# A weight-making step rearranged: an early store, two VectorE steps moved ahead, a cast in front of a wait

## The chip, the cores and the metric

The kernel runs on one core of a Trainium2 chip. TensorE multiplies matrices, VectorE (DVE) and ScalarE (ACT) do element work, GpSimd (POOL) does some element work and issues part of the transfers, SyncE (SP) issues the rest. Each engine runs its own queue in order and waits on semaphores for the others. The metric is device time in microseconds; lower is better.

## The reference

Linear attention with random features (`phi(x) = exp(h - max h)`), and behind it two feed-forward layers over 2304 tokens, of width 512 and inner width 2048:

```python
x = attention(q, k, v, omega)                     # [2304, 512]
h = x @ w_in;  x = (max(h, 0) + alpha * min(h, 0)) @ w_out
h = x @ w2_in; out = max(h, 0)**2 @ w2_out
```

The weights are float64 numbers; the result is float32.

## The kernel before, in words

**Products.** Every float32 matrix is held as two parts, a rounded one (`h`) and the rest (`l`), and a product is three TensorE products of such parts. Tokens are three blocks of 768. The 2048 inner columns are eight pairs `p` of 2 x 128. For a pair, the block products of `x @ w_in` are made with seven products in place of eight (a Strassen-Winograd scheme): the weight blocks A21, A22, A11, A12 and four sums S1 to S4 of them stand as eight columns of `wf1`, products 1, 2, 6, 5, 7, 4, 3 follow each other in `pair` (line 840 is the matmul), and in between stand slices of the second product `y` of the pair before (line 1036). Two PSUM banks called `h` serve the seven products in turn, so the second product of a pair (product 2) can begin only when VectorE's line 878 has read the last one (product 3) of the pair before.

**Making weights.** A pair's weights have to be made before it is used: this goes on beside the first token block, one unit a pair. Unit n stands beside pair n-1 and makes `w_in` of pair n and `w_out` of pair n-1. A `Raw` object is 512 KB of float64 words: POOL fetches it (line 128) into one of three buffers `ms`, ScalarE scales the high words (138) and the low words (146) and puts the sign in (153), VectorE shifts (157) and merges (161) to float32. In unit n the four raw rows are called `a`, `b` (the two rows of `w_in`) and `p`, `q` (those of `w_out`, q the last). A buffer is free for the fetch of the raw row three places on when shift and sign have read it, so `q` is fetched once `a` has been shifted. Then `sums` (179) adds S1, S3, S2, S4, `cast1`/`cast2` (`high`, 244, ScalarE) round, `rest1`/`rest2` (`low`, 247, VectorE) subtract, and `keep` (250, SP's queue) writes both parts to DRAM, since blocks 2 and 3 read them again: 1792 KB for `w_in`, 2 x 512 KB for `w_out` a unit.

**What sets the order.** It is written out by hand: `evenly` puts every step of a unit on one of seven stages (`STEPS`), and stage m's instructions are issued just ahead of product m of the pair. Within an engine this order is final. Work of the products themselves (ACT 865 copies out of PSUM, DVE 878, 883, 889 bend and split) stands between. `APART` places four subtractions of `x` (`apart`, 527, POOL) beside the steps 13 to 16 of the attention's second half.

Of the kernel before, what the change touches and what calls it, by code (L numbers as in the profile page):

```python
# [44 lines left out]

MADE = {3: 1, 4: 2, 5: 3, 6: 4, 7: 5, 12: 6, 13: 8, 14: 9, 15: 10, 16: 11, 17: 12, 18: 14, 19: 16, 20: 18}
CASTS = (7, 8, 9, 10)
APART = {13: 4, 14: 6, 15: 5, 16: 3}
CAST = 11
STAGES, SHORT = 18, 10  # L50
STEPS = (2, 5, 7, 10, 12, 15, 17)
# [10 lines left out]
def tile_performer_moe(ctx, tc, qt, kt, qn, kn, vn, omt, w1i, w1o, al, w2i, w2o, out):  # L62
# [27 lines left out]
    A21, A22, A11, A12, S1, S2, S3, S4 = range(8)  # L90
# [9 lines left out]
    ring = {}  # L100
# [85 lines left out]
    def made():  # L186
# [19 lines left out]
        def merge(raw):  # L206
            raw.merge()
            if raw in raws:
                read_out(raw)

        def read_out(raw):
            raws.remove(raw)
            fetch()
# [35 lines left out]
        def keep(key, which, at, tile, queue=nc.sync):  # L249
            queue.dma_start(out=kept[key][which][:, :, at].bitcast(F32), in_=tile.bitcast(F32))  # L250

            if at in (0, slice(0, 7), slice(5, 7)):
                done.add((key, which))

        f1, f2 = tiles["wf1"], tiles["wf2"]
# [16 lines left out]
        def cast1(key, a0, a1):  # L272
            high(first(key, 0, a0, a1), f1[:, a0:a1])

        def rest1(key, a0, a1):
            low(first(key, 1, a0, a1), f1[:, a0:a1], first(key, 0, a0, a1))
# [8 lines left out]
        def evenly(n, n1, n2, todo):  # L285

            def put(step, *what):
                todo[STEPS[step]] += what

            joined = tiles["joined"], tiles["single"].bitcast(I32)  # L290
            put(0, trail)
            put(1, trail)
            if n1:
                a, b = used[n, 0, 0], used[n, 0, 1]
                put(0, a.scale_high)
                put(1, lambda: a.scale_low(joined[0]), a.sign, a.shift, lambda: read_out(a))
                put(2, lambda: merge(a), b.scale_high, lambda: b.scale_low(joined[1]), b.shift)
                put(3, b.sign, lambda: read_out(b), lambda: cast1(n1, A11, S1))
                put(4, lambda: merge(b), lambda: sums((1, 3)), lambda: sums((2, 4)), lambda: rest1(n1, A11, S1))
            if n2:  # L300
                p, q = (lambda: used[n, 1, 1]), (lambda: used[n, 1, 0])
                put(3, lambda: p().scale_high())
                put(4, lambda: p().scale_low(joined[0]))
            if n1:
                put(4, lambda: cast1(n1, A22, A11))
            if n2:
                put(4, lambda: p().sign(), lambda: p().shift(), lambda: read_out(p()), lambda: q().scale_high())
            if n1:
                put(4, lambda: cast1(n1, S1, S3), lambda: rest1(n1, A22, A11))
                put(5, lambda: rest1(n1, S1, S3))  # L310
            if n2:
                put(5, lambda: q().scale_low(joined[1]), lambda: q().sign(), lambda: merge(p()),
                    lambda: q().shift(), lambda: read_out(q()))
            if n1:
                put(5, lambda: cast1(n1, S3, 8))
            if n2:
                put(6, lambda: cast2(n2, 1))
            if n1:
                put(6, lambda: rest1(n1, S3, 8),
                    lambda: keep(n1, 0, slice(0, 7), ring[n1[1] % 2][0][:, :, A22:]))  # L320
            if n2:
                put(6, lambda: merge(q()), lambda: rest2(n2, 1),
                    lambda: tail.extend([lambda: cast2(n2, 0), lambda: rest2(n2, 0)]))
# [199 lines left out]
    def apart(n):  # L523

        of = {T1: (T3, T1), T3: (T2, T3), T2: (T2, T1), T4: (T4, T2)}[n]
        a, b = (in_place(0, m) for m in of)
        nc.gpsimd.tensor_tensor(out=in_place(0, n), in0=a, in1=b, op=ALU.subtract)
# [561 lines left out]
    for n, (layer, k, turn, p) in enumerate(plan):  # L1089
        lead = plan[n + 1] if n + 1 < len(plan) else None  # L1090
        held[p % 2] = layer, p
        reading = lead and lead[:2] != (0, 0) and held[lead[3] % 2] != (lead[0], lead[3])
        if layer:
            making_room.close()
            values(0)
        fill = enumerate(mm2(*before)) if before else iter(())
        full = []
        first, whole = (layer, k) == (0, 0), n < 2
        if n == 0:
            ask(ENDS[0], None)  # L1100
        steps = stepping.pop() if stepping else plain(p) if whole else pair(layer, p)
        for m, got in enumerate(steps, DRAINED if n == 0 else 0):
            if reading and m in (0, 2):
                read(lead[0], lead[3], 0, m // 2)
            if layer and m == 0:
                for part in GROUPS:
                    read_pair(0, 1, part)
            if first and turn:

                upto((p + 1) * STAGES + STAGES * (m + 1) // (8 if whole else 7) + 1, ENDS[0], None)  # L1110
            elif layer == 0 and k and turn * 7 + m > 3:
                upto(end_of(ENDS[k - 1]) + (end_of(ENDS[k]) - end_of(ENDS[k - 1])) * (turn * 7 + m - 3) // (0, 52, 49)[k],
                     ENDS[k], k)
            elif layer == 0 and k and m == 3:
                ask(ENDS[k], k)
            elif (layer, k, turn) == (0, 1, 0) and m < 2:

                onward(ENDS[0], None)
            for what, operand_ in SPLIT.get((n, m), ()):
                what(0, operand_, in_place)  # L1120
            for blk, at in ((n // NPAIR, turn * 7 + m), (n // NPAIR - 1, NPAIR * 7 + turn * 7 + m)):

                if 0 <= blk < BLOCKS:
                    at -= (NPAIR - 1) * 7
                    for what, operand_ in [*(NEXT if blk else LATER).get(at, ()), *TABLE.get(at, ())]:
                        what((blk + 1) % BLOCKS, operand_)
            for rows in full:
                evacuate(ended, y, rows)
            full = []
            for _ in range(FILL[0 if whole else 1][m]):  # L1130
                part, _ = next(fill, (None, None))
                if turn == 0 and part is not None and part in COMPLETE:
                    full.append(COMPLETE[part])
        for part, _ in fill:
            if turn == 0 and part in COMPLETE:
                full.append(COMPLETE[part])
        for rows in full:
            evacuate(ended, y, rows)
        if turn == 0 and not layer:
            y = [py.tile([P, 512], F32, name=f"y{c}") for c in range(NB // P)]  # L1140
        if reading and lead[0] == 0:
            read(lead[0], lead[3], 1, 1)
            read(lead[0], lead[3], 1, 0)
        before = turn, p, *got, y
        ended = k
# [302 lines left out]
```

## Time and profile before

| | |
|---|---|
| median of 3 runs | 882.21 us (881.02 to 882.24) |
| profiled execution | 880.5 us, span 878.7 us |
| PE busy | 867.7 us (99%) |
| DVE, ACT, POOL busy | 676.5, 520.7, 96.7 us |
| granted TensorE clock | 1.00 over the span, that is 2.4 GHz |
| moved by DMA | 228.76 MB, mean 260 GB/s |

The stretches: attention to about 130 us, the eight pairs of the first token block from there to about 262 us (here the weights are made), then the other blocks and the second layer. PE's busy time is modelled at its ends, so a busy share of 99% doesn't say that matmuls follow at their full pace: the start-to-start distance of matmul rows does.

### The profile page before, as it was taken

The page shows a single profiled execution, that of the slowest core. Times are in us where ns is not written, and L with a number is a line of the kernel's source. Part 1 is how long each engine was busy: PE and PEld are TensorE (multiplying, and loading weights), DVE is VectorE, ACT ScalarE, POOL GpSimd, SP SyncE. Part 2 cuts the span into 40 slices and gives each one's busy share as a digit, 9 for nine tenths or more (in the row PEclk, how much of TensorE's full clock was granted, in tenths as well). Part 3 has the DMA queues.
Part 4 walks back from the last instruction along what each step waited for, and adds up shares of the span by engine and source line. Part 5 has one row for each costly group of instructions (what it writes and reads, how often), then busy time and mean ns, then how long its engine had stood idle before and what let it go on. Part 6 is the DMA issues. An engine that isn't in the chain of part 4 may idle for free.

```text
span 878.7 us, 17471 instructions
## 1 busy us (share of the span) xinstructions
PE 867.7 (99%) x6812; PEld 800.0 (91%) x6812; DVE 676.5 (77%) x1117; ACT 520.7 (59%) x1027; POOL 96.7 (11%) x138
## 2 busy tenths in 40 slices
PE   9999999999999999999999999999999999999998
PEld 7998889978888999989999999998899988999887
DVE  4778996888797777788787874669965699757685
ACT  6889886888776666576676643335523245333442
POOL 6642441111101000001000000000000000000000
PEclk9999999999999999999999999999999999999999
DMA  8544305778846999947999975777697687876873
GB/s 288 181 144 154 110 14 213 267 272 332 289 173 243 331 387 380 380 147 280 395 402 394 359 253 181 252 255 281 239 304 253 207 329 252 284 261 224 303 259 142
DMA packets 86898, 228.76 MB, mean 260 GB/s; under 512 B 6688, under 2 KB 19360, under 8 KB 81824
## 3 DMA queue, kind: packets, MB, share of 16 engines
q1 hardware_dynamic: 77248, 192.21, 61.0%
q0 software_dynamic: 9216, 33.56, 10.9%
q10 hardware_dynamic: 352, 1.87, 0.6%
q8 instruction: 54, 0.88, 0.4%
q14 instruction: 28, 0.23, 0.1%
HBM read 170.47 MB, written 57.15 MB: 259 GB/s over the span
## 4 chain that ended last, share of the span: by engine, by line
PE 68%; DVE 2%; ACT 2%; DMA 1%; issue 0%; DVEq 0%; ACTq 0%
PE h L840 22%; PE y L1036 16%; PE sumc L1227 11%; PE spare L840 10%; PE suma L1227 9%; DMA ms<-in_w1o 1%; DMA x<-in_w2i 0%; PE h L1227 0%; DVE xl L501 0%; DVE w L247 0%; DVE c L883 0%; ACT x L1054 0%; DVE wf L161 0%; DVE gl L889 0%; ACT x L138 0%
## 5 line engine op out<-in xcount | busy, mean ns | idle before, releaser
L840 PE MATMUL h<-xh,w 128*128 128x384 f32 x1016 | 288.2, 338 | 3.8 <-DVE c L878 3.2
L840 PEld LDWEIGHTS h<-xh,w 128*128 128x128 f32 x1016 | 186.3, 188 | 9.1 <-DVE c L878 5.7
L1036 PE MATMUL y<-gh,w 128*128 128x512 f32 (+1 forms) x768 | 175.5, 338 | 1.5 <-DVE w L247 1.2
L840 PE MATMUL h<-xl,w 128*128 128x384 f32 x508 | 170.5, 336 | 0.0
L1036 PEld LDWEIGHTS y<-gh,w 128*128 128x128 f32 x768 | 130.5, 188 | 15.2 <-DVE w L247 3.1
L1036 PE MATMUL y<-gl,w 128*128 128x512 f32 (+1 forms) x384 | 102.4, 337 | 0.0
L1242 ACT CAST gh<-g 128x768 fp32r<-128x768 f32 x72 | 56.9, 833 | 74.1 <-PE suma L1227 33.2
L840 PEld LDWEIGHTS h<-xl,w 128*128 128x128 f32 x508 | 95.5, 188 | 2.0
L840 PE MATMUL spare<-xh,w 128*128 128x384 f32 x336 | 91.0, 334 | 0.0
L1244 DVE TENSOR_TENSOR gl<-g,gh 128x768 fp32r<-128x768 f32 x72 | 65.7, 953 | 14.3 <-PE suma L1227 7.1
L1227 PE MATMUL sumc<-w,gh 128*128 128x512 f32 (+1 forms) x296 | 76.6, 379 | 0.0
L1036 PEld LDWEIGHTS y<-gl,w 128*128 128x128 f32 x384 | 67.1, 188 | 9.6
L840 PEld LDWEIGHTS spare<-xh,w 128*128 128x128 f32 x336 | 61.3, 188 | 0.2
L1227 PEld LDWEIGHTS sumc<-w,gh 128*128 128x128 f32 x296 | 52.8, 188 | 9.3
L613 DVE TENSOR_REDUCE mx<-h 128x8 f32<-128x1024 f32 x36 | 44.0, 1223 | 20.8 <-PE h L600 20.2
L878 DVE SCALAR_TENSOR_TENSOR c<-h,sg_sb,s 128x384 f32<-128x384 f32 x66 | 40.5, 614 | 24.3 <-ACT s L865 13.7
L865 ACT ACTIVATE s<-h,sg_sb 128x384 f32<-128x384 f32 x66 | 38.1, 577 | 31.8 <-PE h L840 31.8
L883 DVE SCALAR_TENSOR_TENSOR c<-c,al_sb 128x768 f32<-128x768 f32 x48 | 48.6, 1013 | 9.9 <-ACT c L865 9.9
L840 PE MATMUL spare<-xl,w 128*128 128x384 f32 x168 | 56.1, 334 | 0.0
L1227 PE MATMUL suma<-w,gh 128*128 128x512 f32 x216 | 52.4, 391 | 0.0
L865 ACT ACTIVATE gh<-c,sg_sb 128x768 fp32r<-128x768 f32 x48 | 45.0, 938 | 7.3 <-DVE c L883 6.9
L889 DVE SCALAR_TENSOR_TENSOR gl<-c,sg_sb,gh 128x768 fp32r<-128x768 f32 x48 | 48.5, 1010 | 0.0
(133 smaller groups left out, 1488.5 us busy)
## 6 DMA issues: line engine op xcount, KB each, us to landing
w<-k SPq DMA_DIRECT2D x99, 512.0 KB, 5.2
w<-k SPq DMA_DIRECT2D x39, 1024.0 KB, 5.1
w<-k SPq DMA_DIRECT2D x26, 896.0 KB, 9.0
k<-ms SPq DMA_DIRECT2D x36, 512.0 KB, 7.4
k<-w SPq DMA_DIRECT2D x7, 1792.0 KB, 6.8
k<-w SPq DMA_DIRECT2D x16, 512.0 KB, 6.5
x<-in_w2i POOLq DMA_DIRECT2D x16, 512.0 KB, 6.7
x<-in_w2o POOLq DMA_DIRECT2D x16, 512.0 KB, 7.2
```

The costliest lines, as they stand in the source:

```text
L613: nc.vector.reduce_max(out=mx, in_=pj, axis=AX.X)
L840: nc.tensor.matmul(out, w[:, u, a, cs], tiles[v, b][:, kc], start=start and kc == 0 and j == 0, stop=stop and kc == 1 and j == 2, skip_gro ...
L865: nc.scalar.mul(out=to, in_=of, mul=sg_sb[:, 2 * p + i:2 * p + i + 1])
L878: nc.vector.scalar_tensor_tensor(out=c[:, ts], in0=b, scalar=sign, in1=s, op0=ALU.mult, op1=ALU.add)
L883: nc.vector.scalar_tensor_tensor(out=c, in0=c, scalar=slope, in1=c, op0=ALU.mult, op1=ALU.max)
L889: nc.vector.scalar_tensor_tensor(out=gl[:, i], in0=c, scalar=sign, in1=gh[:, i].bitcast(F32), op0=ALU.mult, op1=ALU.subtract)
L1036: nc.tensor.matmul(y[a0 // 512][:, a0 % 512:a0 % 512 + a1 - a0], u[:, i, c * P:(c + 1) * P], v[:, i, ts], start=first and j == 0 and a0 % ...
L1227: nc.tensor.matmul(to[c] if v == 3 or banks else to[c][:, :QW], (l if v == 2 else h)[:, r, c * P:(c + 1) * P], both(r) if v == 3 else w[:, ...
L1242: nc.scalar.copy(out=h[:, r], in_=f[:, r])
L1244: nc.vector.tensor_tensor(out=l[:, r], in0=f[:, r], in1=h[:, r].bitcast(F32), op=ALU.subtract)
```

## The change

Four things change. The store of a unit's `w_in` parts is cut in two: columns 0 to 3 (A22, A11, A12) are stored in step 4, as soon as their rests are there, the four sums in step 6. VectorE's merge of row `b` and the first rest come one step sooner (step 3 in place of 4). ScalarE's casts of A22 and of the sums S1, S2 move in front of the scaling of `p`'s low words and of `q`'s high words, and the cast of S3, S4 in front of `q`'s low words. And one `apart` (T4) leaves step 16 of the attention for the first product of pair 1.

```diff
-APART = {13: 4, 14: 6, 15: 5, 16: 3}
+APART = {13: 4, 14: 6, 15: 5}
...
-            if at in (0, slice(0, 7), slice(5, 7)):
+            if at in (0, slice(0, 7), slice(3, 7), slice(5, 7)):
                 done.add((key, which))
...
+            def save(a0, a1):
+                keep(n1, 0, slice(a0, a1), ring[n1[1] % 2][0][:, :, A22 + a0:A22 + a1])
...
-                put(3, b.sign, lambda: read_out(b), lambda: cast1(n1, A11, S1))
-                put(4, lambda: merge(b), lambda: sums((1, 3)), lambda: sums((2, 4)), lambda: rest1(n1, A11, S1))
+                put(3, b.sign, lambda: read_out(b), lambda: cast1(n1, A11, S1), lambda: merge(b),
+                    lambda: rest1(n1, A11, S1))
+                put(4, lambda: sums((1, 3)), lambda: sums((2, 4)), lambda: cast1(n1, A22, A11))
...
-                put(4, lambda: p().scale_low(joined[0]))
-            if n1:
-                put(4, lambda: cast1(n1, A22, A11))
+                put(4, lambda: p().scale_low(joined[0]), lambda: p().sign(), lambda: p().shift(), lambda: read_out(p()))
+            if n1:
+                put(4, lambda: cast1(n1, S1, S3), lambda: rest1(n1, A22, A11), lambda: save(0, 3))
+                put(5, lambda: rest1(n1, S1, S3), lambda: cast1(n1, S3, 8))
             if n2:
-                put(4, lambda: p().sign(), lambda: p().shift(), lambda: read_out(p()), lambda: q().scale_high())
-            if n1:
-                put(4, lambda: cast1(n1, S1, S3), lambda: rest1(n1, A22, A11))
-                put(5, lambda: rest1(n1, S1, S3))
-            if n2:
+                put(4, lambda: q().scale_high())
...
-            if n1:
-                put(5, lambda: cast1(n1, S3, 8))
...
-                put(6, lambda: rest1(n1, S3, 8),
-                    lambda: keep(n1, 0, slice(0, 7), ring[n1[1] % 2][0][:, :, A22:]))
+                put(6, lambda: rest1(n1, S3, 8), lambda: save(3, 7))
...
+            if (n, m) == (1, 0):
+                apart(T4)
```

The later lines of `after` are two lower than before (878 is 876, 865 is 863, 179, 247, 161, 157, 244, 138 stay). On **VectorE**, in the middle of a unit (here the one that makes pair 4; `t,joined` is row a or p, `t,ma` row b or q, `w_0_102` the eight weight columns), before:

```order
L161 ISA wf_100<-t,joined 128x1024
L157 TENSOR_SCALAR t<-ms_2697 128x512
L878 SCALAR_TENSOR_TENSOR c<-h,sg_sb,s 128x384
L161 ISA wf_100<-t,ma 128x1024
L179 TENSOR_TENSOR wf_100<-wf_100 128x256 x4
L247 TENSOR_TENSOR w_0_102<-wf_100,w_0_102 128x512
L157 TENSOR_SCALAR t<-ms_2698 128x512
L247 TENSOR_TENSOR w_0_102<-wf_100,w_0_102 128x256
L247 TENSOR_TENSOR w_0_102<-wf_100,w_0_102 128x512
```

and after the change:

```order
L161 ISA wf_100<-t,joined 128x1024
L157 TENSOR_SCALAR t<-ms_2696 128x512
L161 ISA wf_100<-t,ma 128x1024
L247 TENSOR_TENSOR w_0_102<-wf_100,w_0_102 128x512
L876 SCALAR_TENSOR_TENSOR c<-h,sg_sb,s 128x384
L179 TENSOR_TENSOR wf_100<-wf_100 128x256 x4
L157 TENSOR_SCALAR t<-ms_2697 128x512
L247 TENSOR_TENSOR w_0_102<-wf_100,w_0_102 128x256
L247 TENSOR_TENSOR w_0_102<-wf_100,w_0_102 128x512
```

The merge of b and the first rest now stand ahead of the PSUM reader (878, now 876), and the sums directly behind it. This holds for six units; in the first of them no PSUM reader stands there.

On **ScalarE** at the same place (`ms_2698` and then `ms_2699` are rows p and q; 128x256 is the cast of A22, the 128x512 ones of `w_0_102` those of the sums), before:

```order
L865 ACTIVATE s<-h,sg_sb 128x384
L146 ACTIVATE joined<-ms_2698 128x512
L244 CAST w_0_102<-wf_100 128x256
L153 CAST joined<-ms_2698 128x512
L138 ACTIVATE ms_2699<-ms_2699 128x512
L244 CAST w_0_102<-wf_100 128x512
L865 ACTIVATE c<-h,sg_sb 128x384
L146 ACTIVATE ma<-ms_2699 128x512
L153 CAST ma<-ms_2699 128x512
L244 CAST w_0_102<-wf_100 128x512
L244 CAST w_1_2703<-wf_101 128x512
```

and after it (the buffers' numbers are one lower):

```order
L863 ACTIVATE s<-h,sg_sb 128x384
L244 CAST w_0_102<-wf_100 128x256
L146 ACTIVATE joined<-ms_2697 128x512
L153 CAST joined<-ms_2697 128x512
L244 CAST w_0_102<-wf_100 128x512
L138 ACTIVATE ms_2698<-ms_2698 128x512
L863 ACTIVATE c<-h,sg_sb 128x384
L244 CAST w_0_102<-wf_100 128x512
L146 ACTIVATE ma<-ms_2698 128x512
L153 CAST ma<-ms_2698 128x512
L244 CAST w_1_2702<-wf_101 128x512
```

Each of the three casts of these weights stands one place or more sooner, two of them in front of a scaling that waits for a raw row.

On **SP's queue** the store of the weights (`k_0_2` is pair 2's `w_in`, `k_1` pair 1's `w_out`), before:

```order
L250 DMA k_0_2_67<-w_0_102 256x1x1792
L250 DMA k_1_82<-w_1_2703 256x1x512 x2
L250 DMA k_0_3_68<-w_1_103 256x1x1792
L250 DMA k_2_83<-w_0_104 256x1x512 x2
L250 DMA k_0_4_69<-w_0_102 256x1x1792
```

and after it:

```order
L250 DMA k_0_2_67<-w_0_102 256x1x768
L250 DMA k_0_2_67<-w_0_102 256x1x1024
L250 DMA k_1_82<-w_1_2702 256x1x512 x2
L250 DMA k_0_3_68<-w_1_103 256x1x768
L250 DMA k_0_3_68<-w_1_103 256x1x1024
L250 DMA k_2_83<-w_0_104 256x1x512 x2
```

Six stores of 1792 columns become six of 768 and six of 1024; the bytes are the same.

## Rows read from the trace of the kernel before

**Rows 1.** Who waited for whom over the span: total us, times, longest us.

```profile
ACT ms L138 <- DMA ms<-in_w1o: 6.8, 5, 1.8
...
PE h L840 <- DVE c L878: 3.2, 4, 1.1
...
PE y L1036 <- DVE w L247: 1.2, 5, 0.3
```

**Rows 2.** One pair: us, PE, PEld, DVE, ACT, POOL busy, clock, DMA share, GB/s.

```profile
193.67:211.09 17.42, 16.33 (x92) 14.62 (x91) 15.06 (x28) 15.19 (x26) 2.11 (x4) 1.00 0.81 289
```

**Rows 3.** TensorE's timeline at that pair's start: start us, us, instruction [idle <-releaser].

```profile
193.67 0.33 PE L840 MATMUL h<-xh,w 128*128 128x384 f32 x1
...
194.55 0.34 PE L840 MATMUL h<-xh,w 128*128 128x384 f32 x1
195.74 0.45 PE L840 MATMUL h<-xh,w 128*128 128x384 f32 x1 [0.85 <-DVE c L878]
...
196.90 0.40 PE L1036 MATMUL y<-gh,w 128*128 128x512 f32 x1
197.54 0.74 PE L1036 MATMUL y<-gh,w 128*128 128x512 f32 x3 [0.24 <-DVE w L247]
```

**Rows 4.** VectorE's timeline of the unit before it, and the next unit's first shift.

```profile
187.32 0.62 DVE L878 SCALAR_TENSOR_TENSOR c<-h,sg_sb,s 128x384 f32<-128x384 f32 x1 [1.83 <-ACT s L865]
187.86 0.68 DVE L161 CUSTOM_DVE_ANT_0 wf<-t,ma 128x1024 uint16<-128x1024 uint16 x1
188.57 1.56 DVE L179 TENSOR_TENSOR wf<-wf 128x256 f32<-128x256 f32 x4
...
192.47 0.69 DVE L247 TENSOR_TENSOR w<-wf,w 128x512 fp32r<-128x512 f32 x1 [1.06 <-ACT w L244]
...
195.07 0.61 DVE L878 SCALAR_TENSOR_TENSOR c<-h,sg_sb,s 128x384 f32<-128x384 f32 x1
...
200.39 0.42 DVE L157 TENSOR_SCALAR t<-ms 128x512 int32<-128x512 int32 x1
```

**Rows 5.** ScalarE's timeline of the same unit, and the next unit's row p.

```profile
185.00 0.79 ACT L153 CAST ma<-ms 128x512 f16<-128x512 f32 x1
...
191.25 0.68 ACT L138 ACTIVATE ms<-ms 128x512 f32<-128x512 f32 x1 [1.58 <-DMA ms<-in_w1o]
191.83 0.60 ACT L244 CAST w<-wf 128x512 fp32r<-128x512 f32 x1
192.34 0.58 ACT L865 ACTIVATE c<-h,sg_sb 128x384 f32<-128x384 f32 x1
...
203.55 0.66 ACT L138 ACTIVATE ms<-ms 128x512 f32<-128x512 f32 x1
```

**Rows 6.** GpSimd's timeline: the fetches of q, of the next p, of the next q.

```profile
183.98 0.53 POOL L128 DMA_DIRECT2D ms<-in_w1o  x1 [6.06 <-ACT s L865]
...
194.77 0.53 POOL L128 DMA_DIRECT2D ms<-in_w1o  x1 [2.62 <-ACT w L244]
201.35 0.53 POOL L128 DMA_DIRECT2D ms<-in_w1o  x1 [6.05 <-ACT s L865]
```

**Rows 7.** Queues in 180.2:183.9, 184.9:188 and 188.1:191.3: packets, MB, share.

```profile
q1 hardware_dynamic: 205, 1.47, 96.3%
...
q1 hardware_dynamic: 478, 0.97, 101.6%
...
q0 software_dynamic: 262, 0.97, 81.3%
```

**Rows 8.** Timelines of GpSimd, VectorE and TensorE at step 16 of the attention's second half.

```profile
116.23 1.81 POOL L527 TENSOR_TENSOR x<-x 128x768 f32<-128x768 f32 x1
...
116.94 1.72 DVE L179 TENSOR_TENSOR wf<-wf 128x256 f32<-128x256 f32 x2
...
120.54 0.63 PE L720 MATMUL t<-ident,eq 128*128 128x128 f32 x4 [0.44 <-DVE mx L619]
```

**Rows 9.** VectorE's timeline where T4 is now put.

```profile
144.49 1.02 DVE L883 SCALAR_TENSOR_TENSOR c<-c,al_sb 128x768 f32<-128x768 f32 x1 [1.47 <-ACT c L865]
```

## The prediction

> **What bounds the kernel now.** I read the sum of waits first, then one pair by its busy times, then the timelines of TensorE, VectorE and ScalarE over that pair, and last the transfer queues.
>
> TensorE is busy 99% of the span, so what can be won lies in its few waits. Two kinds of them stand together: line 840 waited four times for VectorE's line 878, 3.2 us in all, and line 1036 five times for a rest of the weights (247), 1.2 us in all [rows 1]. All lie at the starts of pairs 3 to 7 of the first token block, beside which weights are made. The idle time is not the whole cost. In the pair that begins at 193.67 the first six matmuls start 0.176 us apart (193.67 to 194.55 in five steps), the next one 1.19 us later: 1.02 us lost where 0.85 is called idle; and the six matmuls after the wait take 1.16 us to 196.90 in place of 1.06 [rows 3]. So a wait costs its idle time and about 0.27 us. Nine waits: 4.4 + 9 x 0.27 = 6.8 us. That pair lasts 17.42 us [rows 2] and loses 0.85 + 0.24 + 2 x 0.27 = 1.63: its full pace is about 15.8 us.
>
> Why is 878 late? On VectorE the two instructions with idle time before them are 878 at 187.32 (1.83 us, for ScalarE's copy out of PSUM) and the rest of S1, S2 at 192.47 (1.06 us, for ScalarE's cast); from there to the 878 at 195.07, which ends at 195.68, the queue has no gap [rows 4]. The cast was late because on ScalarE it stood behind the scaling of row q, which waited 1.58 us for the transfer [rows 5]; there are five such waits [rows 1]. And q's row is late because of the stores: fetched at 183.98 [rows 6], but in 184.9 to 188 the hardware queue's stores had 101.6% of the engines and the software queue nothing listed beside them; in 188.1 to 191.3 the software queue moved 0.97 MB [rows 7]. q took 191.25 - 183.98 = 7.27 us. The loop closes: the fetch follows the shift of a by 0.96 us (200.39 to 201.35 [rows 4, 6]), and that shift stands at the end of VectorE's full queue.
>
> The Trainium skill (DMA: Bandwidth & Descriptors, Queues, rings and completion order) says that each engine goes round the queues that have work, a packet at a time; q would then have moved at half rate beside the stores. The rows disagree with it here: q's queue got nothing until the stores were drained. By that rule rival B below could not happen; by the rows it can.
>
> **The change part by part.** The sum is made against the profiled execution, 880.5 us (span 878.7 and 1.8 around it); the median of the runs shown is 1.7 us above it, and the gain is taken from that median.
>
> *Merge of b and first rest in front of 878* (six units). Nothing new: two instructions of 0.68 us each [rows 4]. The merge can start when b's sign is in, 185.00 + 0.79 = 185.79 [rows 5]; both are done by 187.2, inside the idle 1.83 us in front of 878 [rows 4]. Cost nothing. If that cover went (ScalarE's copy earlier, or b later), 878 would be late by up to 1.2 us; it frees a bank that TensorE wants three products later, so the pair would still not wait.
>
> *Sums directly behind 878.* They start at 187.86 and not 188.57; four take 1.56 [rows 4], the third (S2) ends at about 189.0, all at 189.4.
>
> *Cast of A22, then of S1, S2, in front of the rows.* ScalarE now waits for VectorE's merge of b and for S2. Queued behind these casts: p's low words and sign, q, the copy `c`. The merge is done (186.5) before ScalarE comes to it; p's low words and sign (0.69 + 0.79) are done at about 189.0, as S2 is. The cast then runs at 189.0 to 189.6 in place of 191.83 to 192.43, inside the 1.58 us that ScalarE spends waiting for q [rows 5]. The rest of S1, S2 comes at 189.4 + 2 x 0.34 (shift of p, rest of A22) = 190.1, not 192.47.
>
> *What is late next.* Let q land as late as now. Then: q's scaling 191.25, `c` directly behind it, done 192.4 (before: 192.92), the bend 883 0.93 us, 878 done at 194.0. TensorE wants it at 194.55 + 0.18 = 194.73: slack 0.7 us, no wait (before: 1.02 us lost). For the second kind of wait: sign of q done at 191.25 + 0.57 + 0.48 + 0.51 + 0.69 + 0.79 = 194.3, VectorE free of the rest of S3, S4 at 194.6, merge of q 0.6, rest of `w_out` done at 195.9. At full pace TensorE wants it at 197.54 - 0.41 - 1.12 = 196.0: slack 0.1, so some of this wait may stay if q lands no sooner. The next shift of a: 883, 878, 889 and a rest (0.93 + 0.53 + 0.92 + 0.60) later, 198.8 in place of 200.39. From q's landing to the next fetch 198.8 + 0.96 - 191.25 = 8.5 us, and 7.27 for the transfer: 15.8 us, just the pair's full pace. So even without the split the loop would hardly hold TensorE.
>
> *The store in two parts.* SP issues six DMAs more (12 in place of 6), same bytes. 1.835 MB at 1.47 MB in 3.7 us [rows 7] is 4.6 us; of these 0.79 MB, 2.0 us, now go at about 191, when the queues are about to be empty, and no longer stand in front of q. So q starts up to 2 us sooner. They stand instead in front of the next b and p. The p row is fetched at 194.77 [rows 6] and scaled at 203.55 [rows 5], 8.8 us later, 7.2 of them left at full pace; alone it needs about 3 us. Bounds for the split: a gain of 2.0 us on q's landing, a loss of 2.0 us on p's; the first helps the thin 0.1 us, the second is covered. DMA busy in a pair is 0.81 x 17.4 = 14.1 us [rows 2]: at 15.8 us a share of 0.89. It fits, without much room.
>
> *T4 moved.* Beside GpSimd's 527 two sums took 1.72 us [rows 8], where four take 1.56 without it [rows 4]: 0.94 us that pushed a maximum, for which TensorE waited 0.44 us [rows 8]. Without it TensorE goes on about 0.5 us sooner, and nothing else is late at that step. At the new place the subtraction runs beside VectorE at about 143.4 to 145.3; there VectorE had been idle 1.47 us before 144.49 [rows 9], so up to 0.94 us more is hidden. Bounds: a gain of 0 to 0.5, a loss of 0 to 0.3; I take 0.5, the size of the wait shown.
>
> Sum: 6.8 + 0.5 = 7.3 us, less 0.3 for what may stay of the second wait: 7.0. 880.5 - 7.0 = 873.5 on the profiled execution, **875.2 us** on the median.
>
> **The rivals.**
>
> B: the late row is no longer q but p. For: the queues serve what came first, and the second part of the store is now issued close behind p's fetch, while the first part holds up b in front of it. If p falls behind the second part (1.05 MB at 0.40 MB/us, 2.6 us) and `w_out` (1.05 MB at 0.97 MB in 3.1 us [rows 7], 3.4 us), it lands some 8.7 us after 194.8 with its own transfer, 1.5 us after it is wanted at full pace. Against: p is fetched before the second part is issued. The price lies between 0 and 1.5 us a pair; at 0.75 the gain is 5 x (1.36 - 0.75) + 0.5 = 3.5 us: 878.7 us. (1.36 is 6.8 over five pairs.)
>
> C: the change doesn't do what it says. ScalarE's new waits and q's landing shift together, 878 is as late as now, and only T4 counts: 881.7 us. For: the loop of 15.8 us leaves no slack if the transfer is slower at a share of 0.89. Against: 2.4 us of VectorE's lateness lie in two idle times which are shown.
>
> D, the slower side: the smaller store rows. A row was 7 KB and is now 3 and 4 KB. 7 KB rows moved 0.40 MB/us, the 2 KB rows of `w_out` 0.31 [rows 7]. Should the new ones move at only 0.20 MB/us, the `w_in` store takes 9.2 us, and with `w_out` (3.4) and four raw rows (2.1 MB at 0.97 MB in 3.2 us [rows 7], 6.9) a pair needs 19.5 us of the queues: 2.3 us over the present mean of about 17.2 (15.8 + 1.36), five times, 11 us: 893 us. It decides from the point where the store takes over 6.9 us (0.27 MB/us). Against: even the 2 KB rows were faster.
>
> **How the numbers follow.** Forecast 0.74, B 0.14, C 0.07, D 0.05. A measurement of this kernel can tell about 0.2%, 1.8 us, from no change: 880.4 and 884.0 are the bounds. The forecast and most of B (0.11) are faster: 0.85; C and the rest of B are the same: 0.10; D is slower: 0.05. The forecast's own range goes from 873.6 (all of 7.3, the small waits that rows 1 leaves out, 0.6 us of runs' spread) to 877. The range for 8 in 10 takes in B: 873.6 to 880.2; outside are C, D and a little below.
>
> **What would show it.** Right: no wait of TensorE for 878 or 247 between 176 and 250, pairs 3 to 7 of 15.8 us; VectorE's idle before 878 in mid-unit shrunk to about 0.6, none of 1 us before the rest of S1, S2; ScalarE's wait for `in_w1o` gone or without a TensorE wait behind it; q's landing under 6 us; the 0.44 us at 120.5 gone. Wrong: B shows as a wait of ScalarE on row p (the first `in_w1o` of a unit) in the fourth product; C as 1 us idle before 878's bank still; D as a DMA share near 1.0 from 160 to 260 and stores over 7 us.

## The result, and the profile after

The kernel after takes 872.46 us (median of 4 runs, 871.88 to 872.83), the kernel before 881.62 beside it (4 runs, 880.87 to 882.24): ratio 0.9896, 95% interval 0.9879 to 0.9913, 9.2 us less. The profiled execution went from 880.5 to 872.57, 7.9 us less where 7.0 were forecast. The forecast of 875.2 us was 2.7 us too high, and the time lies 1.1 us under the low end of its range. In the runs below, single executions lie up to some 7 us above the median of their kernel, most of them at a granted clock of 0.992 to 0.996.

First the sum of waits of the kernel after (engine, line, what it waited for: total us, times, longest). The lines are two lower here: 876 is the 878 of before, 838 the 840, 863 the 865.

```profile
PE h L838 <- ACT c L863: 0.3, 1, 0.3
ACT ms L138 <- DMA ms<-in_w1o: 1.6, 2, 0.9
```

The first row is all that is left of TensorE's waits between 100 and 285 us; those for 878 and 247 are gone, and ScalarE waits for rows of `in_w1o` twice and not five times [rows 1]. The next view is the busy time of each engine in the five pairs 3 to 7 (start:end, us, busy PE, PEld, DVE, ACT, POOL, clock, DMA share, GB/s), of before:

```profile
176.66:262.52 85.86, 81.39 (x452) 72.78 (x451) 74.16 (x125) 71.78 (x119) 8.45 (x16) 1.00 0.74 271
```

and of after:

```profile
176.82:255.46 78.64, 78.64 (x451) 73.32 (x451) 73.06 (x124) 69.86 (x116) 7.91 (x15) 1.00 0.81 288
```

A pair lasts 78.64 / 5 = 15.73 us in place of 17.17, and TensorE is busy all of it. VectorE's work is nearly the same (73.06 and 74.16): what went is its idle time, 85.86 - 74.16 = 11.7 us, now 5.6. Where it went is in VectorE's timeline of one unit (start us, us, instruction, idle before it and what ended that):

```profile
184.15 0.69 DVE L161 CUSTOM_DVE_ANT_0 wf<-t,ma 128x1024 uint16<-128x1024 uint16 x1 [0.59 <-ACT ma L153]
184.76 0.68 DVE L247 TENSOR_TENSOR w<-wf,w 128x512 fp32r<-128x512 f32 x1
185.68 0.62 DVE L876 SCALAR_TENSOR_TENSOR c<-h,sg_sb,s 128x384 f32<-128x384 f32 x1 [0.24 <-ACT s L863]
186.21 1.54 DVE L179 TENSOR_TENSOR wf<-wf 128x256 f32<-128x256 f32 x4
187.68 0.42 DVE L157 TENSOR_SCALAR t<-ms 128x512 int32<-128x512 int32 x1
188.01 1.02 DVE L247 TENSOR_TENSOR w<-wf,w 128x256 fp32r<-128x256 f32 x2
...
191.00 0.61 DVE L876 SCALAR_TENSOR_TENSOR c<-h,sg_sb,s 128x384 f32<-128x384 f32 x1
...
192.73 0.68 DVE L247 TENSOR_TENSOR w<-wf,w 128x512 fp32r<-128x512 f32 x1
```

The 1.83 us before the mid-unit 878 [rows 4] now hold the merge of b and the first rest, with 0.59 and 0.24 left; the 1.06 before the rest of S1, S2 are gone (188.01, where two rests stand in one row, has none). The 876 that TensorE wants at the pair's start, the 878 at 195.07 of before [rows 4], is the one at 191.00, done at 191.61. TensorE's pair starts at 192.37, and its seventh matmul, the first that needs 876, is the second of the two that begin at 193.25:

```profile
192.37 0.33 PE L838 MATMUL h<-xh,w 128*128 128x384 f32 x1
193.25 0.52 PE L838 MATMUL h<-xh,w 128*128 128x384 f32 x2
```

It starts at 193.44, 1.8 us after 876 is done. The last row of VectorE is the rest of `w_out`, done at 193.41. On ScalarE and GpSimd the same unit reads:

```profile
187.33 0.62 ACT L244 CAST w<-wf 128x512 fp32r<-128x512 f32 x1
188.59 0.69 ACT L138 ACTIVATE ms<-ms 128x512 f32<-128x512 f32 x1 [0.64 <-DMA ms<-in_w1o]
189.17 0.58 ACT L863 ACTIVATE c<-h,sg_sb 128x384 f32<-128x384 f32 x1
```

```profile
182.05 0.53 POOL L128 DMA_DIRECT2D ms<-in_w1o  x1 [5.41 <-ACT joined L153]
```

The cast of S1, S2 (187.33) runs in front of q's scaling (188.59), which comes 6.54 us after q's fetch (182.05) and not 7.27 [rows 5, 6]. T4's addition is here:

```profile
143.39 1.87 POOL L525 TENSOR_TENSOR x<-x 128x768 f32<-128x768 f32 x1
```

and TensorE's 0.44 us at 120.54 [rows 8] are gone.

Set beside each other matmul by matmul (start of the same one in both traces), the span's 7.9 us come out so: 0.53 from T4's place, 7.2 from pairs 3 to 7, 0.74 from two waits about 279.3 and 280.9, 0.36 at the tail; given back are 0.47 about 22 us, 0.22 about 161.5 and 0.26 late in the program. The first two of the three differ between executions of one kernel too: the control below (e5) stands 0.6 us behind before at 162.

### The profile page after: what moved, and what is told of

Read it like the earlier page. It is cut to its first block, busy times and chain, and to the rows that moved or that the text cites. A ratio compares the mean times of both kernels' runs of the same rounds, so it can differ in the third digit from the quotient of the medians.

```text
span 870.8 us, 17509 instructions
## 1 busy us (share of the span) xinstructions
PE 865.3 (99%) x6812; PEld 801.1 (92%) x6812; DVE 676.0 (78%) x1117; ACT 520.5 (60%) x1027; POOL 96.8 (11%) x138
## 4 chain that ended last, share of the span: by engine, by line
PE 97%; ACT 2%; issue 0%; DVE 0%; ACTq 0%
PE h L838 30%; PE y L1034 23%; PE sumc L1227 11%; PE spare L838 10%; PE suma L1227 9%; PE h L598 4%; PE o L644 2%; PE t L605 2%; PE t L718 2%; PE o L750 2%; PE t L737 1%; PE t L592 1%; ACT e L623 1%; PE h L1227 0%; ACT gh L863 0%
## 5 line engine op out<-in xcount | busy, mean ns | idle before, releaser
L1034 PEld LDWEIGHTS y<-gh,w 128*128 128x128 f32 x768 | 130.8, 188 | 11.7
L1227 PE MATMUL sumc<-w,gl 128*128 128x256 f32 x280 | 48.5, 282 | 0.0
```

Source lines behind the costliest of these rows:

```text
L1034: nc.tensor.matmul(y[a0 // 512][:, a0 % 512:a0 % 512 + a1 - a0], u[:, i, c * P:(c + 1) * P], v[:, i, ts], start=first and j == 0 and a0 % ...
L1227: nc.tensor.matmul(to[c] if v == 3 or banks else to[c][:, :QW], (l if v == 2 else h)[:, r, c * P:(c + 1) * P], both(r) if v == 3 else w[:, ...
```

## The experiments

Medians in us, each beside runs of the kernel before on the same chip; "pair" is a fifth of pairs 3 to 7 in the profiled execution, "VectorE" its busy time in the five and "idle" the rest.

| kernel | median (lowest, highest, runs) | ratio [95%] | pair | VectorE | idle |
|---|---|---|---|---|---|
| before | 881.62 (880.87, 882.24, 4) | 1 | 17.17 | 74.16 | 11.70 |
| e4 VectorE's move | 880.64 (879.20, 883.42, 11) | 0.9999 [0.9989, 1.0010] | 16.98 | 73.97 | 10.95 |
| e1 split | 878.91 (876.67, 884.59, 11) | 0.9983 [0.9966, 0.9999] | 16.90 | 73.94 | 10.58 |
| e3 casts | 876.93 (876.35, 877.89, 5) | 0.9958 [0.9945, 0.9971] | 16.34 | 73.01 | 8.71 |
| e8 split, casts, T4 | 876.26 (875.75, 876.71, 6) | 0.9939 [0.9918, 0.9961] | 16.31 | 73.03 | 8.50 |
| e2 casts, VectorE's move, T4 | 875.42 (874.21, 882.67, 11) | 0.9946 [0.9928, 0.9963] | 16.13 | 72.32 | 8.31 |
| e9 split, VectorE's move | 875.82 (874.67, 878.07, 9) | 0.9937 [0.9917, 0.9956] | 15.97 | 74.11 | 5.73 |
| after: all | 872.46 (871.88, 872.83, 4) | 0.9896 [0.9879, 0.9913] | 15.73 | 73.06 | 5.58 |

VectorE has 72.3 to 74.2 us of work in five pairs, whichever kernel it is; at TensorE's full pace five pairs take 78.64. So it may be idle for about 1.1 us a pair, and before it was for 2.3, nearly all of it in two waits (of the five pairs, with what ScalarE waited for):

```profile
DVE c L878 <- ACT s L865: 7.4, 4, 1.9
DVE w L247 <- ACT w L244: 3.4, 4, 1.3
ACT ms L138 <- DMA ms<-in_w1o: 5.5, 4, 1.8
```

The idle column alone would prove nothing, since a span is work plus idle time by definition; what shows that the waits set the pair is what happened to them as the parts were put in singly and in twos.

**e1, the split alone.**

```
-if at in (0, slice(0, 7), slice(5, 7)):
+if at in (0, slice(0, 7), slice(3, 7), slice(5, 7)):
...
+put(4, ..., lambda: save(0, 3))
-put(6, lambda: rest1(n1, S3, 8), lambda: keep(n1, 0, slice(0, 7), ...))
+put(6, lambda: rest1(n1, S3, 8), lambda: save(3, 7))
```

> Before, with the store of w_in alone cut in two; all instructions of VectorE and ScalarE stand as before. Theory L (a loop: the stores hold up q's raw row, ScalarE waits for it, the cast of S1, S2 behind it holds up VectorE, and 878 and the rest of w_out hold up TensorE): q's fetch takes some 2 us less than the 6.5 to 7.3 of before, ScalarE's wait for it goes, the cast comes about 1.5 us sooner, the rest of S1, S2 about 1.06 us: the wait for 878 (0.7 to 1.1 us idle a pair) goes or nearly, about half of the wait for 247 stays. 4.5 to 6 us faster than before. Rival S (the stores don't hold q up, engines' order alone counts): within 1 us of before, q's fetch as long as before.

Only 1.5 to 2 us came. The waits in the five pairs:

```profile
DVE c L880 <- ACT s L867: 7.3, 4, 1.8
DVE w L247 <- ACT w L244: 2.3, 1, 2.3
PE h L842 <- DVE c L880: 2.2, 2, 1.4
PE y L1038 <- DVE w L247: 1.1, 5, 0.3
```

The wait for the cast went in three units of four; in the other one, the second, q came later than ever (scaled 8.5 us after its fetch), and it cost TensorE 1.44 us at once. The wait of 1.8 us in front of 878 stays in all four. From issue to landing q took 5.3, 8.5, 5.4 and 6.1 us in the four units, and 7.2, 6.5, 7.5 and 7.0 before: some 2 us less in two units, 0.9 in one, and 2 us more in one. Why that one was late stays open. Pair by pair (start of the same matmul) the five take 17.25, 16.76, 18.07, 16.22 and 16.22 us: the 4.5 to 6 us of the expectation stand in the last two (five such pairs would give 4.8), while a late q held the others (6.6 us from issue to landing in the unit ahead of the first, 6.5 in before, and the 8.5 beside the second). b, in front of which a part of the store now stands, took 5.9 us and not 3.9, which nothing felt.

**e2, everything but the split.** After with `save(0, 3)` left out and `save(0, 7)` at the end.

> The changed kernel with the w_in store in one piece in step 6 again, all else as changed. Theory L by hand: q lands as late as before (6.5 to 7.3 us after its fetch), but the cast stands in front of it and the loop of 15.8 us just fits the pair: TensorE's waits for 878 gone, 0.1 to 0.3 us a pair may stay before 247; 0 to 2 us slower than the changed kernel, 7 to 9 faster than before. Rival (the split carries the gain): 5 us or more slower than the changed kernel.

It is 3.0 us slower than after: more than the 2 us of theory L, less than the 5 of its rival. In the traces, matmul by matmul, 2.0 of it lie in the five pairs and 1.0 about 272 to 274 us of after, where before has its waits at 279.3 and 280.9. Two of TensorE's waits are left that are long enough to be listed, 0.3 and 0.2 us, yet a pair is 16.13 us. VectorE has found a third thing to wait for, the late row itself, which took 7.6 to 8.4 us from issue to landing:

```profile
DVE t L157 <- ACT ms L138: 4.1, 4, 1.5
DVE wf L161 <- ACT ma L153: 2.5, 4, 0.6
ACT ms L138 <- DMA ms<-in_w1o: 8.0, 4, 2.5
```

**e3, ScalarE's order alone.**

```
+put(4, lambda: cast1(n1, A22, A11) if n1 else None)
 put(4, lambda: p().scale_low(joined[0]))
-put(4, lambda: cast1(n1, A22, A11))
-put(4, lambda: p().sign(), lambda: p().shift(), lambda: read_out(p()), lambda: q().scale_high())
+put(4, lambda: p().sign(), lambda: p().shift(), lambda: read_out(p()))
 put(4, lambda: cast1(n1, S1, S3), lambda: rest1(n1, A22, A11))
-put(5, lambda: rest1(n1, S1, S3))
+put(5, lambda: rest1(n1, S1, S3), lambda: cast1(n1, S3, 8))
+put(4, lambda: q().scale_high())
...
-put(5, lambda: cast1(n1, S3, 8))
```

With these lines the three casts come sooner; VectorE's order, the store and T4 stay.

> Before, with only ScalarE's three casts moved in front of the scalings of p and q; VectorE's order, the single store and T4 as before. Theory L: S2 is done at 189.74 in the unit shown, the cast at 190.3 and not 191.8, the rest of S1, S2 at 191.3 and not 192.5, so 878 ends about 194.4 where TensorE wants it at 194.7: the wait for 878 goes, 0.2 us a pair stays before 247. 4.5 to 6 us faster than before. Rival (both VectorE's and ScalarE's moves are needed together): 2 us or less faster.

3.7 us by the ratio, under the 4.5 to 6 expected; the largest part of the three taken singly. The wait for the cast is gone, the one of 878 not, and VectorE's other share (L247) reaches TensorE only twice:

```profile
DVE c L875 <- ACT s L862: 7.6, 4, 2.0
PE y L1033 <- DVE w L247: 0.5, 2, 0.2
```

**e4, VectorE's move alone.**

```
-put(3, b.sign, lambda: read_out(b), lambda: cast1(n1, A11, S1))
-put(4, lambda: merge(b), lambda: sums((1, 3)), lambda: sums((2, 4)), lambda: rest1(n1, A11, S1))
+put(3, b.sign, lambda: read_out(b), lambda: cast1(n1, A11, S1), lambda: merge(b),
+    lambda: rest1(n1, A11, S1))
+put(4, lambda: sums((1, 3)), lambda: sums((2, 4)))
```

> Before, with only VectorE's merge of b and first rest one step sooner. Theory L: the sums come 0.7 us sooner, but the cast of S1, S2 still stands behind q's raw row on ScalarE; VectorE's idle time only moves from in front of 878 to in front of the rest of S1, S2 (1.06 becomes about 2.3 us). Within 0.7 us of before. Rival (VectorE's load is the bound, so filling its idle 1.83 us is what counts): 4 us or more faster than before.

As expected, no gain that can be told from noise. The five pairs' waits say why:

```profile
DVE w L247 <- ACT w L244: 8.0, 4, 2.2
DVE c L879 <- ACT s L866: 0.9, 4, 0.2
```

The wait before 878 went from 7.4 to 0.9 us, and the wait for the cast took it over, from 3.4 to 8.0: the sums were ready sooner and stood before a cast that waits for q.

**e5, before once more.**

> The kernel before, unchanged: a control. It settles how far a profiled execution may stand from the median of its kernel. Theory O (the profiled 880.5 us of before was an ordinary execution, so that nothing was to be added for a median of after): the median here is 880.5 to 881.6 us, the ratio 1.000 with one inside its interval, and the profiled time within 1.0 us of the median on either side; its attention pairs 3 to 7 lose the same 4.4 to 5.5 us of TensorE to the late casts and sums as before. Theory P (a profile is always about 1.7 us below the median): the profiled time is 1.4 to 2.0 us below the median again.

881.26 us (879.57 to 886.17, 12 runs), ratio 1.0005 [0.9984, 1.0026]; its profiled execution is 881.41, 0.15 above its median. That is theory O. That the 880.5 of the first profile stood 1.7 under the median of the three runs shown with it was chance. Over the other kernels here the profiled execution lies between 1.4 us under its median (e4) and 0.7 above it (e1).

**e6, T4's place alone.**

```
-APART = {13: 4, 14: 6, 15: 5, 16: 3}
+APART = {13: 4, 14: 6, 15: 5}
...
+            if (n, m) == (1, 0):
+                apart(T4)
```

> The kernel before with the one table entry moved alone: T4's addition leaves the chunk that stood third in pair 2 and is issued in pair 1. Theory L (the step as it was priced): TensorE's idle 0.44 us at 120.5 us is gone; of it about 0.2 us comes back as a longer wait about 161 us, where after has one too; pairs 3 to 7 keep their waits, so 880 to 881 us, 0.2 to 0.6 us under before, ratio 0.9993 to 0.9998. Theory N (the addition was hidden anyway): idle of the same size at another place within pair 1 or 2 and the time of before within 0.2 us. If it is more than 2 us faster, T4 had a part in the 7 us that is not seen in the pairs.

880.31 us (879.08 to 881.56, 11 runs), ratio 0.9984 [0.9969, 0.9998]. In the trace the idle time at 120.5 is gone and 0.4 us with it, but 0.34 come back about 161.4, where the control loses 0.14 too; behind that the trace stands 0 to 0.6 us ahead of before, since pairs differ between executions. That is theory L. The ratio's middle says 1.4 us, but its interval begins at 0.2.

**e7, unit 2 sooner.** After, with one line changed:

```
-upto((p + 1) * STAGES + STAGES * (m + 1) // (8 if whole else 7) + 1, ENDS[0], None)
+upto((p + 1) * STAGES + STAGES * min(m + 1, 7) // 7 + 1, ENDS[0], None)
```

> The kernel after, with one number changed: beside the first pair of attention the vector work of unit 2 is spread over 7 of the pair's steps and not over 8, so that its last casts come about one step (2 us) sooner. Theory L (what waits remain about 161 and 166 us are unit 2's last sums coming just too late): the waits of TensorE for ScalarE's casts of line 863 there (0.7 us in two places in the profile of after) go, and 0.4 to 0.9 us of the time with them: 871.6 to 872.2 us. Theory N (ScalarE runs into the raw rows, which come no sooner): ScalarE waits 1 to 2 us for DMA in pair 1, its softmax work is held up behind that, and the time is that of after or up to 1 us above.

873.22 us (872.86 to 873.68, 4 runs), 0.8 above after. Theory L falls, and N's mechanism too, since ScalarE waited for no row there: in its order more casts now stand in front of `c` (162.18 against 160.95), and the one wait became longer:

```profile
162.79 0.44 PE L838 MATMUL h<-xh,w 128*128 128x384 f32 x1 [1.86 <-ACT c L863]
```

**e8, after without VectorE's move.** The diff of e4 undone in the kernel after.

> The kernel after, with one of its parts undone: the second row's addition and the first remainder on VectorE stand a step later again, in the place that they had before. Theory L (VectorE's move matters only where the casts come early, since it then makes room ahead of the sums that TensorE waits for): the wait of VectorE's sums (line 247) for ScalarE's rounded sums stays short, TensorE idles 0.2 to 0.4 us more in each of pairs 3 to 7: 1 to 2 us more than after, 873.5 to 874.5 us. Theory N (the part does nothing in any company, as it did nothing alone): within 0.5 us of after, 872 to 873 us. Theory S (the move is what let the rest be hidden): 3 us or more above after.

876.26 us: 3.8 above after, theory S. In the traces 2.9 of it lie in the five pairs and 1.0 about 272 to 274 us of after; the rest stands ahead of the pairs, where executions of one kernel differ. The part that is worth nothing alone is worth no less than the others when they are there: taken out of after, it costs 2.9 us in the pairs, the split 2.0 (e2), the casts 1.2 (e9), though the times of the three kernels cannot be told apart. What is left is one wait a unit, and its follower on TensorE:

```profile
DVE c L876 <- ACT s L863: 7.4, 4, 1.8
PE y L1034 <- DVE w L247: 1.0, 4, 0.3
```

**e9, split and VectorE's move.** The diffs of e1 and e4 together.

> The kernel before with the store cut in two and VectorE's two instructions moved, but ScalarE's order (casts behind the late raw row) as before and T4 where it was: the one pair of the three parts that has not been run. Theory M (the time of a pair is the later of two chains, q's row and VectorE's sums, and the cast that joins them must stand free of both): with the casts still behind q's scaling, VectorE's move shows as idle time before the rest of S1, S2 as it did alone (some 10 us in the unit's pairs), and the time is that of the split alone, 878 to 880 us. Theory S (the move is worth 3 to 4 us in any company that has made q sooner, as the kernel after against the one without the move): 875 to 876 us.

875.82 us, theory S. Pair by pair it takes 16.93, 15.74, 15.72, 15.74 and 15.72 us, after 15.72 to 15.74 in each: with these two parts alone four pairs of five run at full pace with the casts in their old order. The first does not, since in the unit ahead of it q still takes 6.3 us from issue to landing and VectorE waits 1.76 us for the cast. Theory M was wrong on the size of what is left: with q landing 5.2 to 5.9 us after its issue (before 6.5 to 7.5) the wait for the cast is 0.6 us a unit, where it had been 2.0 in e4.

```profile
DVE w L247 <- ACT w L244: 2.4, 4, 0.8
ACT ms L138 <- DMA ms<-in_w1o: 2.5, 4, 0.8
```

**e10 and e11, the store written later.** e10 is the kernel before with these lines; e11 does the same to the kernel after, with its store in one piece.

```
+put(3, lambda: stores.pop(0)() if stores else None)
...
-put(6, lambda: rest1(n1, S3, 8), lambda: keep(n1, 0, slice(0, 7), ...))
+put(6, lambda: rest1(n1, S3, 8), lambda: stores.append(lambda: keep(n1, 0, slice(0, 7), ...)))
```

> The kernel before with nothing changed but the time at which the whole input weights of a unit are stored: 1.84 MB in one piece, issued behind the fetch of b in the next unit's fourth step (about 191.7 in the pair that was read) and not at the unit's end (178.9). Theory Q (q's row is late because this store stands in front of it): q lands 3.3 to 4.5 us after its issue instead of 6.0 to 6.4, ScalarE's waits for in_w1o of 6.8 us nearly go, line 878 is no longer waited for, and pairs 3 to 7 lose 0 to 2 us, not 5 to 7: 875 to 877 us; p lands later, 5 to 7 us after its issue, which is covered. Theory V (VectorE's full queue is what makes 878 late, and q only comes to stand there): q lands sooner, yet the time falls by less than 2 us, 879 to 881 us.

> The kernel after with its store in one piece again and as late as in the run above (behind the fetch of b in the next unit). If q's delay by the store is all that the split cures, this does the same: 871.9 to 873.0 us, the kernel after's time, with q landing 3.5 to 4.5 us after its issue. If the three parts need the first store part where it is (the halves spread over the pair), p or b comes late behind 1.84 MB in one piece: ScalarE waits for in_w1o or in_w1i in the fourth product, 874 to 876 us. If the pairs run at full pace with less of a queue than after has, the two small waits about 161 and 166 may go too: 871.5 us.

881.07 us (879.60 to 887.39, 12 runs; 1.0002 [0.9984, 1.0021]) and 876.26 (875.43 to 877.81, 6 runs; 0.9938 [0.9914, 0.9962]). Neither answers its question. The stores leave SyncE at the same places of a unit as before (178.63 and 195.85; before 178.94 and 196.31), and q lands 6.7 to 7.4 us after its issue (before 6.5 to 7.5). On SyncE nothing but stores stands in this stretch; each goes when its data is ready, wherever it is written. So e10 repeats before and e11 repeats e2 (876.26 and 875.42).

**e12, the store behind GpSimd.** As e10, with `nc.gpsimd` as the queue of that store.

> The kernel before with its whole store of the input weights (1.84 MB) put into GpSimd's queue, in front of the fetch of b in the next unit: the two runs e10 and e11 left it where it was, since SyncE issues a store as soon as its data is ready, wherever it is written; GpSimd's queue keeps it back until b's fetch. Three waits of VectorE in a pair of the kernel before are named: 1.85 us for ScalarE's copy (line 878), 0.85 for the cast of S1, S2 (247); a pair can hold about 1.1 us of idle VectorE at TensorE's full pace. Theory Q (the store is what makes q late, and q what makes the cast late): q lands 3.2 to 4.5 us after its issue, ScalarE's wait of 5.5 us in five pairs for in_w1o goes, VectorE's wait for the cast with it, the wait of 1.85 us stays: the pair is then about that of the kernel with the casts alone (16.3 us, 877 us), 876 to 878.5 us. If b or p, which now come behind the store, are late, ScalarE shows it as waits for in_w1i or for the first in_w1o of a unit, and the gain is smaller: 878.5 to 881 us. Theory V (q is not late because of the store): q still lands 6 us after its issue, 880 to 882 us.

876.23 us (875.28 to 879.27, 9 runs), ratio 0.9945 [0.9928, 0.9962], a pair of 16.25 us: theory Q in the time, the pair and the waits, with q landing 4.6 to 4.9 us after its issue where 3.2 to 4.5 were expected. GpSimd's timeline shows the store (line 250) at its new place:

```profile
183.00 0.53 POOL L128 DMA_DIRECT2D ms<-in_w1o  x1 [6.05 <-ACT s L867]
185.09 0.53 POOL L128 DMA_DIRECT2D ms<-in_w1i  x1 [1.56 <-ACT ma L153]
185.61 0.71 POOL L250 DMA_DIRECT2D k<-w  x1
190.63 0.54 POOL L128 DMA_DIRECT2D ms<-in_w1i  x1 [4.31 <-DVE w L247]
```

and the waits of the five pairs hold neither ScalarE's for in_w1o nor VectorE's for the cast; what stays is

```profile
DVE c L880 <- ACT s L867: 7.4, 4, 1.9
PE y L1038 <- DVE w L247: 1.1, 5, 0.3
```

q is scaled at 188.55, 5.55 us after its fetch, without a wait. So the store was what made q late, and q what made the cast late; that is shown. And curing q wholly gives 4.8 us by the ratio, where putting the cast in front of it gives 3.7 (e3); the intervals overlap, and the pairs are 16.25 and 16.34: both take away the same wait.

## Why the prediction was right and where it failed

*The bound.* Right: VectorE's two idle times in a unit become TensorE's wait at the pair's start. With the wait for the cast gone (e3, e8, e12) a pair is 16.25 to 16.34; with the wait before 878 gone the other takes over its time (e4), and a pair is 16.98; with both gone it is 15.73.

*The pace.* 15.8 us was forecast, 15.73 measured. Each wait costing its idle time and 0.27 us held too: pairs 3 to 7 gave 7.2 us where the nine waits were put at 6.8, and a tenth, named below, is 0.3.

*Cost nothing.* The merge and the first rest do lie inside the 1.83 us, now 0.83 idle; right. What the step left out is what they are worth: taken by itself "sums directly behind 878" was a link in a chain, but without it the rest gives 3.8 us less (e8). Singly the three parts give 0.1, 1.5 and 3.7 us by their ratios and T4 0.4 to 1.4, 5.7 to 6.7 in all; together they give 9.2, and the noise of such a sum is nearly as large as that difference. What is clear lies in the twos: split and VectorE's move give 0.46 us a pair singly and 1.20 together (e9), split and casts 1.10 singly and 0.86 together (e8).

*What is late next.* The slacks were put too small. Where 0.7 us were forecast for 878, 1.8 are there (done at 191.61, wanted at 193.44); for the rest of `w_out`, forecast at 0.1, it is 1.3: done at 193.41 in after, and the matmul that waited at 197.54 before starts at 194.71. The step had let q land as late as before, and q came 0.7 us sooner in this unit. So the 0.3 us held back "for what may stay of the second wait" were wrong, none of it stayed; a fifth and smaller 878 wait at 212.3, which the rows of waits over 0.2 us each did not list, went as well (0.3 us), and two small ones about 280 (0.74 us) had been left out of the sum; only the range's low end allowed for them. These make the profiled gain 7.9 and not 7.0.

*The loop of 15.8 us without the split* came out at 16.13 (e2), with VectorE waiting for the row itself, 1.0 us a unit: the loop had been closed with 7.27 us for q's transfer, and it took 7.6 to 8.4. It did hold TensorE, by 0.4 us a pair, so the sentence that it "would hardly" do so was too weak; the split is worth 3.0 us on top of the rest.

*The store in two parts.* "So q starts up to 2 us sooner" was too much on the mean: its first packet came 1.0 us sooner in the unit shown, and from issue to landing it took 6.5, 5.9, 5.6 and 6.8 us in the four units, 0.85 less than before. So the sign "q's landing under 6 us" came true in two units of four. b and p landed later, as foreseen, without harm. My expectation for e1 took q's gain for the same in every unit and was missed by 3 us where q was late.

*T4.* 0.5 us forecast; 0.53 at its old place in the kernel after and 0.4 alone, of which about 0.2 and 0.34 come back about 161.

*The step that failed* is the last: "the median of the runs shown is 1.7 us above it, and the gain is taken from that median". No such offset is there: the kernel after's profiled execution (872.57) lies 0.1 from its median, and the control's 0.15 from its own. Of the miss of 2.7 us, 1.8 are this offset and 0.9 the under-counted waits: on the profile alone the forecast was 873.5. Three runs had given the median; in the later comparisons, with 14 to 28 runs of before, it was 880.9 to 881.6, so that the profiled 880.5 stands 0.4 to 1.1 below it. Told from median to median, 7.0 us of gain were forecast and 9.2 came: 0.9 are the under-counted waits, and the rest is that the profile on which the sum was made was itself a quick execution. The range was built on the shifted value with 1.6 us below it, and missed for that.

*The rivals.* B (p late in q's place): not seen, ScalarE has no wait for p in after, though p took 4.8 to 6.3 us from issue to landing and not 3.5 to 3.8; where the queues hurt it was q once more, in one unit of e1. C fell with the result itself: 878 is late no more. D fell with the store's own rate. The hardware queue of the kernel after in 181:182, where its rows are 4 KB, and in 190:191, where they are 3 KB and raw rows move beside them (packets, MB, share of 16 engines):

```profile
q1 hardware_dynamic: 106, 0.43, 105.3%
...
q1 hardware_dynamic: 70, 0.22, 88.7%
```

That is 0.41 and 0.25 MB per us of full share (divide the bytes by the share of the time); rows of 7 KB had 1.47 MB in 96.3% of 3.7 us, 0.41 [rows 7]. The store's 1.05 and 0.79 MB then take 2.6 + 3.2 = 5.8 us; D needed over 6.9.

## What to carry to other kernels

Take the span of a stage, subtract the busy time of the engine next in line, and compare with the same difference at the first engine's full pace: that is the idle time the second may have (here 1.1 us a pair). Where it has several waits beyond that, the gains of single edits don't add: the next wait can take over what one frees, so that a part that measures nothing by itself (e4) is worth 2.9 us in company (e8), and two edits that cure the same wait give less together than singly. Try them together before one is thrown out. And forecast the median from the profiled execution and the rows, not with an offset of a few runs.

## What was not expected of the hardware

- In these traces q's fetch through GpSimd's queue, issued behind running stores, waits until nearly all of them are through, with the split too. In the kernel after q is issued at 182.05; the queues in 182:185 hold no packet of it, and in 185:188 all of it and a part of the next row stand beside the last of the stores:

```profile
q1 hardware_dynamic: 529, 1.18, 100.7%
```

```profile
q0 software_dynamic: 229, 0.87, 85.2%
q1 hardware_dynamic: 108, 0.19, 16.3%
```

  By the packets' records its first packet came 3.1 us after the issue (2.2 and 2.6 in the next two units), 4.1 before, and 1.2 for a row p that finds the queues free. VectorE's own work beside the fetch is not what holds it up: before, VectorE stood idle from 185.49 to 187.32 [rows 4] while q waited from 183.98 to 188.12, and it worked without a gap beside p's 1.2 us. The split took 0.79 MB, some 2 us, from in front of q, and about half of that came out as a sooner landing. The Trainium skill (DMA: Bandwidth & Descriptors, Queues, rings and completion order) states that a DMA engine takes turns between the queues it has work for, packet by packet; these rows of q do not show that. Where a row and a store are issued together, the row at 188.64 and the store at 188.46 in after, the two queues do share, with 0.60 and 0.64 MB in 190 to 194 us; what makes the difference is open.
- A store on an engine that does nothing else there is not moved by moving it in the program (e10, e11); through an engine whose queue holds it back it is (e12).
